# Attention values: query tiles outside and the two key tiles inside, with rows of V packed at 388 bytes

## The chip, the cores and the metric

One core of a Trainium2 chip runs the whole program. The metric is device time in microseconds (us), the median of repeated runs. A run's time is a little longer than the span of its profile, which goes from the first to the last instruction.

## What is computed

Inputs are bf16. There are 2048 query rows of width D = 640, 32 heads of width 192 with their own K and V of 2048 rows, and an FFN of width 1536.

```python
def _A_ref(x, k_cache, v_cache, wq, wo):
    q = (x @ wq).reshape(B, Sq, H, Dh).transpose(0, 2, 1, 3)
    scores = jnp.einsum("bhqd,bhkd->bhqk", q, k_cache) * (Dh ** -0.5)
    p = _softmax(scores, axis=-1)
    o = jnp.einsum("bhqk,bhkd->bhqd", p, v_cache)
    return o.transpose(0, 2, 1, 3).reshape(B, Sq, H * Dh) @ wo

xn = _layernorm(x)
s = _A_ref(xn, k_cache, v_cache, wq, wo)
g = _silu((_silu(xn @ w1) * (xn @ w3)) @ w2)
return x + s * g
```

## The kernel before

The program has a start (layer norm of x, turning it and the first K onto the contraction axis), a long attention part of some 1630 us, and an end (the rest of the FFN, then the product with wo for each of 16 query tiles). The order of instructions on each engine is the order in which the kernel text issues them.

The attention part walks a list of units, `stream`: 32 heads h, in each 4 query blocks qb of 512 queries, in each 8 units p of 256 keys; 1024 units in all. The loop at L653 issues for unit n the scores of unit n + 2 and then the values of unit n, so TensorE always has the scores of two units ahead in PSUM (`st2`) and in SBUF (`pT2`). At p = 0 it first issues the projection of one query block of the next head (`project`, L424: 20 matmuls).

- Scores (`emit_scores`, L487 and L488): six matmuls of 512 columns, two at a time: one on the upper 64 rows of the array and one on the lower 64, each into its own PSUM bank. ScalarE then takes exp of the 128 x 1024 result into `pT2` (L490): keys on partitions, and on the free axis two key tiles t of 512 queries each.
- Values (`values`, L503 to L527): for the two key tiles t and the four query tiles j of 128, and for the two row halves r of the array, one matmul at L516: stationary operand a 64 x 128 piece of `pT2`, moving operand 64 rows of V with 193 columns (192 of V and a column of ones, whose product is the softmax denominator), output the 193 columns of query tile j in `obanks[r]`. These are 16 matmuls in 8 pairs; the two of a pair (r = 0, 1) sit on different rows of the array and run together. `obanks[r]` is two PSUM banks: query tiles 0 and 1 lie in the first, 2 and 3 in the second. Each query tile gathers 16 products (8 units, two key tiles) in each row half. After the eighth unit of a block VectorE copies `obanks[0]` out (L525), adds `obanks[1]` (L526), and later divides by the denominator into `ostage` (L533).

V of a head lives in one of two SBUF tiles `vts[h % 2]`. A partition holds 16 key rows, one after the other. In the kernel before, each row has a place of 256 elements (512 bytes), of which 193 are used. The loads (`load_v`, L283): head 0's V comes in two halves, one from ScalarE's queue and one from SyncE's (L289); from head 1 on two DMAs a head on SyncE's queue (L292), one for the rows that go with t = 0 and one for t = 1, issued for head h + 2 when head h is through. Each row is a piece of 384 bytes. The column of ones is set once (L299).

SBUF tiles of the attention part are laid one behind the other in the order of their pools: `vts`, then `xnS`, `W`, `qA`, `qB`, `qC`, `pT2`, `ostage`, `pt`, `osum` and the layer norm's. When the part is over, the tiles of the end (`t`, `a`, L703 and L705, among them) take over that memory, and the first instruction that writes there waits for what was there before.

Of the kernel before, what the change touches and what calls it, by code (L numbers as in the profile page):

```python
# [11 lines left out]
BF16 = mybir.dt.bfloat16  # L12
# [3 lines left out]
P = 128  # L16
DH = 192
# [111 lines left out]
def _kernel_impl(  # L129
# [22 lines left out]
    NKT = SK // P  # L152
# [39 lines left out]
    vtp = att.enter_context(tc.tile_pool(name="vtp", bufs=1))  # L192
# [14 lines left out]
    xnS = xsp.tile([P, DC, SQ], BF16, name="xnS")  # L207
    x_all = fw.tile([P, WX], BF16, tag="xw", name="x_all")
    x_sb = x_all[:, 0:NQT * D].rearrange("p (t d) -> p t d", d=D)
    vts = [vtp.tile([P, NKT, 256], BF16, name=f"vt{i}") for i in range(2)]  # L210
    loads = {}

    def load_x(g, t0=0, t1=4, queue=nc.sync):
# [289 lines left out]
    def values(n):  # L503

        h, qb, p = stream[n]
        if p == 0:
            for r in range(2):
                obanks[r] = ps_o.tile([P, 1024], F32, tag=f"ob{r}", name=f"obank{r}")
        vt = loads[h]["vt"]
        pT2 = exps.pop(n)  # L510
        for t in range(2):
            for j in range(4):
                start = p == 0 and t == 0 and j % 2 == 0
                stop = p == NPAIR - 1 and t == 1 and j % 2 == 1
                for r in range(2):
                    nc.tensor.matmul(obanks[r][:, j * 256:j * 256 + DH + 1],  # L516
                                     lhsT=pT2[r * 64:(r + 1) * 64, t * 512 + j * P:t * 512 + (j + 1) * P],
                                     rhs=vt[r * 64:(r + 1) * 64, 2 * p + t, 0:DH + 1], start=start, stop=stop)
        if p < NPAIR - 1:
            return  # L520
        if h % HG == 0 and qb == 0:
            ostages[0] = stp.tile([P, NQT, HG * DH], BF16, tag="ostage", name="ostage")
        ov = [obanks[r][:].rearrange("p (j w) -> p j w", j=4)[:, :, 0:DH + 1] for r in range(2)]
        osum = osp.tile([P, 4, DH + 1], F32, tag="osum", name="osum")
        nc.vector.tensor_copy(out=osum[:], in_=ov[0])  # L525
        nc.vector.tensor_tensor(out=osum[:], in0=osum[:], in1=ov[1], op=ALU.add)  # L526
        osums[0] = osum  # L527
# [125 lines left out]
    for n, (h, qb, p) in enumerate(stream):  # L653
        if p == 0 and n > 0:
            if h + 1 < H:
                project(h + 1, qb)
            else:
                ffn_open(qb)
        if h == 0 and qb == 0 and p == 3:
            project(1, 0)  # L660
        if h == 0 and qb + 1 < NQB and p == (5 if qb == 0 else 4):
            project0(qb + 1)
        scores(n + 2)
        values(n)
        if p == 0 and n > 0:
            finish_block(n - 1)
        if p == (5 if h == 0 else 2) and h < 2 * NPIG:
            swiglu(h, qb)
        if p == 4 and h + 1 == H:
            ffn_close(qb)  # L670
        if h == 0:
            first_head(qb, p)
# [22 lines left out]
    for qb in range(NQB):  # L695
        qs = slice(qb * 512, (qb + 1) * 512)
        for fl in range(FL2 // P):
# [5 lines left out]
            t = fsb.tile([P, 512], BF16, tag="t", name="t")  # L703
# [19 lines left out]
    for i in range(NQT):  # L723
# [5 lines left out]
        for b, (c0, c1) in enumerate(DP):  # L729
            t = fsb.tile([P, 512], BF16, tag="ft", name="ft")  # L730
# [30 lines left out]
@with_exitstack  # L761
def kernel(
    ctx: ExitStack,
    tc: tile.TileContext,
    A_x: bass.AP,
    A_k_cache: bass.AP,
    A_v_cache: bass.AP,
    A_wq: bass.AP,
    A_wo: bass.AP,
    B_x: bass.AP,  # L770
    B_w1: bass.AP,
    B_w3: bass.AP,
    B_w2: bass.AP,
    out: bass.AP,
):
    _kernel_impl(ctx, tc, A_x, A_k_cache, A_v_cache, A_wq, A_wo, B_w1, B_w3, B_w2, out)
# [30 lines left out]
```

## Time and profile before

| what | value |
|---|---|
| median of 3 runs | 1939.32 us (1939.16 to 1939.7) |
| the profiled execution | 1939.16 us, its span 1937.4 us (1.76 us lie around it) |
| TensorE (matmuls) | busy 1927.5 us, 99% of the span |
| ScalarE | busy 1180.1 us, 61% |
| VectorE | busy 654.4 us, 34% |
| GpSimd | busy 282.4 us, 15% |
| values matmuls, L516 | 16384, 243 ns each from issue to end |
| V loads, L289 and L292 | 64 DMAs, median 6.0 us from issue to landing on SyncE's queue |

Matmuls are pipelined: the 243 ns of one is its way through the array. What sets the time is the step from one start to the next. Those steps are read from the chain of waits, which gives each group of matmuls the time until the next group starts, or from counts of matmuls in short windows.

### The profile page before, as it was taken

The numbers are of one execution on the slowest core, as the hardware profiler recorded it, in microseconds if no ns is written. First come the engines' busy times: TensorE is split into PE (matmuls) and PEld (weight loads), VectorE is DVE, ScalarE is ACT, GpSimd is POOL, SyncE is SP. The second block draws the span as 40 slices with busy tenths as digits, with TensorE's granted clock in tenths as the row PEclk, the third lists the DMA queues.
The fourth block names the chain that finished last, engine by engine and source line by source line (L and its number), as shares of the span: only waits on it lengthen the run. The fifth ranks groups of instructions, "written<-read, shape, count | busy, mean of one in ns | idle before, by whom it ended". The sixth has DMA issues, their size and how long they took to land.

```text
span 1937.4 us, 59668 instructions
## 1 busy us (share of the span) xinstructions
PE 1927.5 (99%) x27273; PEld 1316.9 (68%) x27281; DVE 654.4 (34%) x997; ACT 1180.1 (61%) x1278; POOL 282.4 (15%) x501
## 2 busy tenths in 40 slices
PE   9999999999999999999999999999999999999998
PEld 6666666666666666666666666666666666577776
DVE  7333333333333333333333333333333334521111
ACT  6667676767676767776777777677767677210000
POOL 3111111111111111111111111111111110000000
PEclk9999999999999999999999999999999999999999
DMA  8643433323333434363434343434334220937872
GB/s 179 131 101 66 100 68 80 88 60 89 59 88 64 98 64 98 68 162 68 101 64 101 69 101 69 101 64 100 69 67 97 59 68 2 251 76 138 152 151 62
DMA packets 394643, 178.98 MB, mean 92 GB/s; under 512 B 341616, under 2 KB 382832, under 8 KB 394384
## 3 DMA queue, kind: packets, MB, share of 16 engines
q1 hardware_dynamic: 371136, 125.32, 31.5%
q0 software_dynamic: 19472, 45.71, 10.1%
q8 instruction: 215, 3.52, 0.8%
q10 hardware_dynamic: 3776, 4.06, 0.7%
q14 instruction: 44, 0.36, 0.1%
HBM read 52.82 MB, written 27.79 MB: 42 GB/s over the span
## 4 chain that ended last, share of the span: by engine, by line
PE 98%; DMA 1%; DVE 1%; ACT 0%; SPq 0%; issue 0%; DVEq 0%; ACTq 0%
PE obank L516 35%; PE st L487 33%; PE ps L424 14%; PE ps_s L111 11%; PE ps_f L727 3%; PE ps_gu L701 1%; DMA x_all<-in_A_x_dram 1%; PE st L488 1%; PE ps L410 0%; DVE stats L316 0%; ACT KW L277 0%; PE pst L354 0%; ACT xnT L356 0%; DVE qA L429 0%; SPq L289 0%
## 5 line engine op out<-in xcount | busy, mean ns | idle before, releaser
L490 ACT ACTIVATE pT<-st 128x1024 bf16<-128x1024 f32 x1024 | 1046.2, 1022 | 250.9 <-PE st L488 235.3
L516 PEld LDWEIGHTS <-pT 64*128 64x128 bf16 x16384 | 711.6, 94 | 241.9 <-ACT pT L490 0.2
L516 PE MATMUL obank<-vt,pT 64*128 64x193 bf16 x16384 | 849.6, 243 | 0.0
L487 PE MATMUL st<-qC,KW 64*128 64x512 bf16 x2046 | 605.8, 376 | 0.1
L525 DVE COPY osum<-obank 128x772 f32<-128x772 f32 x128 | 123.1, 962 | 787.1 <-PE obank L516 787.1
L488 PE MATMUL st<-qB,KW 64*128 64x512 bf16 x1024 | 385.2, 376 | 0.0
L487 PE MATMUL st<-qA,KW 64*128 64x512 bf16 x1022 | 384.5, 376 | 0.4 <-ACT pT L490 0.3
L488 PE MATMUL st<-qC,KW 64*128 64x512 bf16 x1022 | 384.5, 376 | 0.0
L488 PE MATMUL st<-qA,KW 64*128 64x512 bf16 x1022 | 384.4, 376 | 0.0
L487 PEld LDWEIGHTS <-KW 64*128 64x128 bf16 x3068 | 278.5, 94 | 153.7 <-issue 2.1
L424 PE MATMUL ps<-xnT,W 64*128 64x512 bf16 x1280 | 297.2, 376 | 0.0
L424 PE MATMUL ps<-xnS,W 64*128 64x512 bf16 x1280 | 296.3, 376 | 0.0
L488 PEld LDWEIGHTS <-KW 64*128 64x128 bf16 x3068 | 278.8, 94 | 0.7 <-issue 0.6
L377 POOL DMA_DIRECT2D qC<-qA x124 | 65.4, 527 | 1284.5 <-DVE rl_all L532 1268.3
L430 ACT CAST qB<-ps 128x512 bf16<-128x512 f32 x131 | 76.7, 585 | 228.2 <-PE ps L424 222.7
L111 PE MATMUL ps_s<-wo_sb,oT 128*128 128x384 bf16 (+3 forms) x1535 | 208.8, 299 | 0.1
L424 PEld LDWEIGHTS <-W 64*128 64x128 bf16 x2560 | 123.1, 94 | 121.1
L111 PEld LDWEIGHTS <-oT 128*128 128x128 bf16 x1536 | 148.3, 98 | 60.5
L526 DVE TENSOR_TENSOR osum<-osum,obank 128x772 f32<-128x772 f32 x128 | 122.7, 959 | 13.4
L533 DVE TENSOR_TENSOR ostage<-osum,rl_all 128x768 bf16<-128x768 f32 x128 | 122.6, 958 | 6.2 <-DMA o_scr<-ostage 1.9
L465 DVE SCALAR_TENSOR_TENSOR hT<-pt,qB 64x512 bf16<-64x512 bf16 x64 | 43.8, 684 | 197.4 <-ACT pt L464 197.4
L429 DVE CAST qA<-ps 128x512 bf16<-128x512 f32 x131 | 90.6, 691 | 25.0 <-PE ps L410 7.2
(84 smaller groups left out, 623.7 us busy)
## 6 DMA issues: line engine op xcount, KB each, us to landing
o_scr<-ostage SPq DMA_DIRECT2D x16, 1536.0 KB, 10.6
vt<-in_A_v_cache_dram SPq DMA_DIRECT2D x63, 384.0 KB, 6.0
qC<-qA POOLq DMA_DIRECT2D x248, 64.0 KB, 1.9
qC<-qB POOLq DMA_DIRECT2D x124, 64.0 KB, 2.4
wo_sb<-in_A_wo_dram POOLq DMA_DIRECT2D x1, 7680.0 KB, 37.3
W<-in_A_wq_dram POOLq DMA_DIRECT2D x32, 160.0 KB, 3.6
W<-in_B_w_dram POOLq DMA_DIRECT2D x32, 80.0 KB, 3.3
W<-in_A_wq_dram POOLq DMA_DIRECT2D x32, 80.0 KB, 2.9
```

Source lines behind the costliest of these rows:

```text
L111: nc.tensor.matmul(ps[:, 0:w], lhsT=oT[:, k, :], rhs=wo_sb[:, k, c0:c1], start=(k == 0), stop=(k == OC - 1))
L377: nc.gpsimd.dma_start(out=qC[0:64, half, :], in_=qAB[half][64:P, :])
L424: nc.tensor.matmul(ps[:, r * 512:(r + 1) * 512], lhsT=W[rows, j, :], rhs=xs[rows, j // 2, qs], start=(j == 0), stop=(j == 2 * DC - 1))
L429: a = nc.vector.tensor_copy(out=qAB[0][:], in_=ps[:, 0:512])
L430: b = nc.scalar.copy(out=qAB[1][:], in_=ps[:, 512:1024])
L487: nc.tensor.matmul(st2[:, 0:512], lhsT=ka, rhs=qa, start=r == 0 and nr == 3, stop=r == nr - 1)
L488: nc.tensor.matmul(st2[:, 512:1024], lhsT=kb, rhs=qb2, start=r == 0 and nr == 3, stop=r == nr - 1)
L490: nc.scalar.activation(out=pT2[:], in_=st2[:], func=ACT.Exp, scale=att_scale)
L516: nc.tensor.matmul(obanks[r][:, j * 256:j * 256 + DH + 1], lhsT=pT2[r * 64:(r + 1) * 64, t * 512 + j * P:t * 512 + (j + 1) * P], rhs=vt[r ...
L525: nc.vector.tensor_copy(out=osum[:], in_=ov[0])
L526: nc.vector.tensor_tensor(out=osum[:], in0=osum[:], in1=ov[1], op=ALU.add)
L533: nc.vector.tensor_tensor(out=ostage[:, qb * 4:qb * 4 + 4, hg * DH:(hg + 1) * DH], in0=osum[:, :, 0:DH], in1=rl.unsqueeze(2).to_broadcast( ...
```

## The change

Two edits. `vts` is allocated with 194 elements a row (388 bytes) where it had 256 (512 bytes). In `values` the loops over query tiles j and key tiles t change places: all that belongs to one query tile is issued together, first with key tile 0, then with key tile 1. The inner loop over r, the operands and the number of the matmuls stay; `start` and `stop` still fall on the first and the last matmul into each bank.

```diff
-    vts = [vtp.tile([P, NKT, 256], BF16, name=f"vt{i}") for i in range(2)]
+    vts = [vtp.tile([P, NKT, DH + 2], BF16, name=f"vt{i}") for i in range(2)]
```
```diff
-        for t in range(2):
-            for j in range(4):
+        for j in range(4):
+            for t in range(2):
                 start = p == 0 and t == 0 and j % 2 == 0
                 stop = p == NPAIR - 1 and t == 1 and j % 2 == 1
                 for r in range(2):
```

In the built programs the two tiles of V take 2 x 6208 bytes a partition in place of 2 x 8192, and the tiles behind them in SBUF lie 3968 bytes lower. The instructions of every engine stand in the same order as before, but for the order of the eight pairs. Three waits differ. In the first unit of each of heads 1 to 31 the wait for the load of the t = 1 rows stands on the second pair of matmuls; it stood on the fifth. The first ACTIVATE of L704 also waits for five earlier loads of weights into `W`, and the first instruction of L706 for four, because `t` and `a` now lie where `W` was.

## The prediction

> **What bounds the kernel now.** I read the page first: its engine shares, its clock row and its chain by line.
>
> ```profile
> PE 1927.5 (99%) x27273; PEld 1316.9 (68%) x27281; DVE 654.4 (34%) x997; ACT 1180.1 (61%) x1278; POOL 282.4 (15%) x501
> PEclk9999999999999999999999999999999999999999
> PE 98%; DMA 1%; DVE 1%; ACT 0%; SPq 0%; issue 0%; DVEq 0%; ACTq 0%
> PE obank L516 35%; PE st L487 33%; PE ps L424 14%; PE ps_s L111 11%; PE ps_f L727 3%; PE ps_gu L701 1%; DMA x_all<-in_A_x_dram 1%; PE st L488 1%; PE ps L410 0%; DVE stats L316 0%; ACT KW L277 0%; PE pst L354 0%; ACT xnT L356 0%; DVE qA L429 0%; SPq L289 0%
> ```
>
> TensorE is the bound from end to end, at its full granted clock, and the line that the change reorders holds 35% of the chain: nothing waits in front of it. So the question is whether a values unit (16 matmuls) takes longer or shorter. The costliest groups confirm that these matmuls stand idle for nothing:
>
> ```profile
> L516 PEld LDWEIGHTS <-pT 64*128 64x128 bf16 x16384 | 711.6, 94 | 241.9 <-ACT pT L490 0.2
> L516 PE MATMUL obank<-vt,pT 64*128 64x193 bf16 x16384 | 849.6, 243 | 0.0
> ```
>
> Third, the chain in order of time in the middle of the attention part (start, length, what):
>
> ```profile
> 903.03 0.67 PE obank L516 x16
> 903.70 0.21 PE st L487
> ...
> 904.35 0.67 PE obank L516 x16
> 905.01 0.21 PE st L487
> ...
> 905.66 0.67 PE obank L516 x16
> ```
>
> A unit repeats every 1.31 us: three rounds of scores and 0.67 us for 8 pairs of values, 83 ns a pair. Fourth, one unit looked into: windows that all begin at 902.80 us and end ever later, with the matmuls of L516 counted in brackets behind TensorE's busy time.
>
> ```profile
> 902.80:902.96 0.16, 0.09 (x4) 0.09 (x4) 1.00 0.00 0
> 902.80:903.04 0.24, 0.17 (x6) 0.17 (x5) 1.00 0.00 0
> 902.80:903.13 0.33, 0.26 (x8) 0.26 (x8) 1.00 0.00 0
> 902.80:903.21 0.41, 0.34 (x10) 0.34 (x10) 1.00 0.23 50
> 902.80:903.30 0.50, 0.43 (x12) 0.43 (x12) 1.00 0.43 98
> ```
>
> Each 0.08 to 0.09 us brings one more pair. In this order the output bank changes behind the second and sixth pair and, between the fourth and fifth, both the bank and the row of V; no step is longer. From the start times of the trace, averaged over 1021 units, the second matmul of a pair starts 3.5 ns behind the first and the next pair 79.9 ns behind that; the step over the change of row is 79.87, the others 79.85 to 79.89. A pair costs 83.3 ns.
>
> **The change part by part.** *Order of the pairs, values.* Removed and added: nothing; 16 matmuls and 16 weight loads a unit stay. Three things move. (a) The row of V now changes at every pair and not once: 0 by the step just shown. (b) The output bank changes once inside a unit, not three times: 0 by the same row. (c) A query tile's two key tiles are now added into the same 193 PSUM columns in consecutive pairs, 83.3 ns apart; before, three other pairs lay between. The kernel has rows for back-to-back sums into the same columns: the last output tile's narrow piece at L111 adds 48 products of 128 columns, all into the same place. Windows of it:
>
> ```profile
> 1930.00:1931.00 1.00, 1.00 (x21) 1.00 (x19) 1.00 0.00 0
> 1930.00:1932.00 2.00, 2.00 (x39) 2.00 (x37) 1.00 0.00 0
> ```
>
> The second microsecond brings 18 matmuls: 55.6 ns each, narrower and closer than 83.3, and with no stall. That piece uses the whole array and not its halves; the scores do use the halves, add three times into one place and also run at their 215.8 ns a round. So (c) is 0. Upper bound: if a sum had to wait until the former one is through (243 ns in place of 83.3), 160 ns on 4096 of the 8192 pairs would be 655 us; the 128-column row (219 ns each, 55.6 apart) speaks against it, and I take 0. Weight loads (94 ns, in pairs on two halves) step through `pT2` in another order and stay hidden under the matmuls.
>
> *Pitch of V.* What can a row starting at a multiple of 388 bytes cost the moving operand? No matmul of this trace streams from such a start, so the price is bounded. The steps give the stream's grain: 215.8 ns for 512 columns and 55.8 for 128 (from the start times) make 0.4167 ns a column and 2.5 ns fixed. 193 columns would be 82.9; measured 83.3, which is 194. I read this as two columns, 4 bytes, at a time, 0.83 ns; 388 is a multiple of 4, so no row needs one more. Low end 0: there is nothing to gain, since pairs already run at the step of a 194-column stream. High end: one more grain on each pair, 8192 x 0.83 = 6.8 us. I take 0, the grain being the nearest row, and keep 6.8 for the range.
>
> [...]
>
> *The V loads.* The same 64 DMAs of the same 384-byte pieces, now onto packed rows. From head 2 on V is loaded a whole head (50.7 us) ahead and lands in about 6 us; head 1's is issued at 60.7 us, lands by about 67 and is read from 75 us: 7 us of cover. If a load took 8 us longer, TensorE would stand in front of head 1 for one. The first half of head 0's V is issued at 6.39 us, lands 7.1 us later, and is read at 16.02: 2.5 us of cover. The tight place is the second half:
>
> ```profile
> 12.43 1.18 SPq L289 DMA_DIRECT2D vt<-in_A_v_cache_dram  x1
> 13.65 1.56 SPq L214 DMA_DIRECT2D x_all<-in_A_x_dram  x1
> 21.97 0.89 DVE L316 BATCH_NORM_STATS2 stats<-x_all 128x6 f32<-128x320 bf16 x2 [0.60 <-DMA x_all<-in_A_x_dram]
> 23.71 0.73 PE L354 MATMUL pst<-ident_bf,xn 128*128 128x128 bf16 x10 [0.75 <-DVE qA L429]
> 25.04 0.83 PE L516 MATMUL obank<-vt,pT 64*128 64x193 bf16 x16
> ```
>
> V itself lands at 20.3 us and is first read at 25.04. But x's third group is queued behind it on SyncE; VectorE waits for that at 21.97, the cast of L429 stands behind VectorE's wait, and TensorE's transposes behind the cast. Every microsecond by which V is slower arrives there. Its 64 pieces on each of 16 DMA engines took 22 ns for most pieces of this size in the records and 42 to 48 for the slowest twentieth, so the bounds are 0 and, were all slow, 64 x 22 = 1.4 us. I take 0.3, nearer to the plain pieces.
>
> *Waits and addresses.* In 31 units the wait for the t = 1 rows stands three pairs (0.25 us) earlier on TensorE, with all of its stream queued behind it. The load is over by 8 us (head 1) or some 40 us (later heads): 0; uncovered it would be 31 x 0.25 = 7.8 us. The new waits of L704 and L706 near 1647 us are for loads whose last was issued at 1588.6 and took 3.4 us: 0. The tiles that lie 3968 bytes lower keep 64-byte starts, and the rows of their instructions have no reason to change: 0. The memset of the ones is one of 72 ns for each tile, as before.
>
> Sum: 1939.16 (its span 1937.4 and 1.76 around it) + 0 + 0 + 0.3 = 1939.46; the profiled execution lies 0.16 below the median of the runs, which gives 1939.6.
>
> **The rivals.** *1, the other side: a misaligned row start costs every values pair a fixed slot.* Place: the moving operand's stream at L516, on the chain. Price 0.83 ns a pair and 6.8 us in all, 1946.1; two grains would give 1953. For it: no aligned row can refute it, and 35% of the chain would pay. Against it: the grain of 4 bytes. It decides from 0.48 ns a pair (3.9 us over 8192). *2: sums into the same columns stall when they follow each other in half-array mode.* Only the second pair of each query tile would pay: one fixed slot of 2.5 ns on 4096 pairs is 10.2 us, 1949.5. Against it stand L111 and the scores. *3: faster.* If bank changes cost something that the steps hide, say the spread of 0.04 ns between them on two changes of 1024 units, it is 0.1 us; to pass 0.2% it would need 3.9 us, while all that TensorE stands idle is 9.9 us (1937.4 - 1927.5), most of it before head 0's second block, where the change can only delay. *4: the change doesn't do what it says.* The order does change in the built program, and the pitch too; what doesn't follow is that anything on the chain cares. That is the forecast itself. Within it, a start delayed by the full 1.4 us gives 1940.9.
>
> **How the numbers follow.** A measurement here can tell about 0.2% (3.9 us) from no change. Forecast, no change, 1937.5 to 1942: 0.62. Rival 1: 0.25 and rival 2: 0.07, nearly all above 0.2%. Faster by more than 0.2%: 0.06. So faster 0.06, same 0.62, slower 0.32. The range goes down to 1937.5 and up to 1947.5: it takes in the one-grain price and leaves out the larger prices of rivals 1 and 2 (about 0.13) and the faster case (0.06).
>
> **What would show it.** In the changed profile: units every 1.31 us and 0.67 us for 16 matmuls in the chain; a pair step of 83.3 ns, evenly spaced. Rival 1: a longer step on all eight pairs, 84.1 ns for one grain, or on rows with certain offsets. Rival 2: long and short steps in turn, the long one in front of each query tile's second key tile. Start: VectorE's wait for x at 21.97 us moved by the slower V pieces. The forecast is wrong if the pair step moves by 0.5 ns or more, or if the chain shows something other than TensorE in the attention part.

## The result and the profile after

The changed kernel takes 1947.25 us (median of 6 runs, 1946.97 to 1948.81) against 1939.39 for the kernel before (6 runs): a ratio of 1.0042, 95% interval 1.0029 to 1.0055. That is 7.9 us slower. The profiled execution has a span of 1945.2 us, 7.8 more than before.

The page names the same bound as before, and the same shares:

```profile
PE 1935.1 (99%) x27273; PEld 1323.2 (68%) x27281; DVE 654.4 (34%) x997; ACT 1180.2 (61%) x1278; POOL 282.6 (15%) x501
PEclk9999999999999999999999999999999999999999
PE 98%; DMA 1%; DVE 1%; ACT 0%; SPq 0%; issue 0%; DVEq 0%; ACTq 0%
L516 PE MATMUL obank<-vt,pT 64*128 64x193 bf16 x16384 | 857.7, 243 | 0.0
```

TensorE's busy time grew by 7.6 us, at the same clock and with the same number of matmuls; what used to wait for it waits longer (ScalarE's exp at L490 242.1 us in all, 235.3 before). A matmul of L516 still takes 243 ns from issue to end, so that figure hides the change. The chain in order of time shows it as a longer period of the blocks. Before:

```profile
75.25 2.16 PE ps L424 x20
87.93 2.16 PE ps L424 x20
100.60 2.16 PE ps L424 x20
```

After:

```profile
88.11 2.16 PE ps L424 x20
100.84 2.16 PE ps L424 x20
```

Each such row opens a query block with its projection. A block took 12.67 us and takes 12.73; 0.06 us on each of 128 blocks is the 8 us. Inside a unit, the same count of L516 in windows with one beginning (902.20 us, after):

```profile
902.20:902.34 0.14, 0.09 (x4) 0.09 (x3) 1.00 0.00 0
902.20:902.42 0.22, 0.17 (x4) 0.17 (x4) 1.00 0.00 0
902.20:902.43 0.23, 0.18 (x6) 0.18 (x6) 1.00 0.00 0
902.20:902.51 0.31, 0.26 (x8) 0.26 (x7) 1.00 0.00 0
902.20:902.59 0.39, 0.34 (x8) 0.34 (x8) 1.00 0.00 0
902.20:902.60 0.40, 0.35 (x10) 0.35 (x10) 1.00 0.00 0
```

The second pair has started by 902.34 and the third has not by 902.42; the fourth has by 902.51 and the fifth not by 902.59. Windows in steps of 10 ns are too coarse to say more; by their start times the eight pairs of this unit lie 83, 87, 83, 87, 81, 87 and 82 ns apart. The steps are uneven now. Averaged over the units of heads 1 to 30, from the start times (ns from the start of a pair to the start of what follows it; the last column is the mean of the three rounds of scores that come next):

```
pair          1      2      3      4      5      6      7      8     sum   scores
before      83.3   83.4   83.3   83.3   83.4   83.3   83.3   83.3   666.7   215.8
after       83.3   87.5   82.5   86.2   82.5   86.1   82.5   86.1   676.8   215.2
```

Pairs 2, 4, 6 and 8 are those with key tile 1. They take 2.8 to 4.2 ns more; every step behind a slow one, the scores included, takes some 0.7 to 0.8 ns less. The values of a unit lose 10.1 ns and its scores win 2.0 back: 8.1 ns on 1024 units, 8.3 us. The projections win some 0.2 ns on each of their 10 rounds a block, 0.3 us in all. That makes 8.0, against 7.8 measured. The start, the end and all waits off TensorE have no part in it.

### The profile page after: what moved, and what is told of

Read it like the earlier page. It is cut to its first block, busy times and chain, and to the rows that moved or that the text cites. A ratio compares the mean times of both kernels' runs of the same rounds, so it can differ in the third digit from the quotient of the medians.

```text
span 1945.2 us, 59672 instructions
## 1 busy us (share of the span) xinstructions
PE 1935.1 (99%) x27273; PEld 1323.2 (68%) x27281; DVE 654.4 (34%) x997; ACT 1180.2 (61%) x1278; POOL 282.6 (15%) x501
## 4 chain that ended last, share of the span: by engine, by line
PE 98%; DMA 1%; DVE 1%; ACT 0%; SPq 0%; issue 0%; DVEq 0%; ACTq 0%
PE obank L516 35%; PE st L487 33%; PE ps L424 14%; PE ps_s L111 11%; PE ps_f L727 3%; PE ps_gu L701 1%; DMA x_all<-in_A_x_dram 1%; PE st L488 1%; PE ps L410 0%; DVE stats L316 0%; ACT KW L277 0%; PE pst L354 0%; ACT xnT L356 0%; SPq L289 0%; DVE qA L429 0%
## 5 line engine op out<-in xcount | busy, mean ns | idle before, releaser
L490 ACT ACTIVATE pT<-st 128x1024 bf16<-128x1024 f32 x1024 | 1046.2, 1022 | 257.7 <-PE st L488 242.1
L516 PEld LDWEIGHTS <-pT 64*128 64x128 bf16 x16384 | 717.7, 94 | 242.3 <-ACT pT L490 0.2
L516 PE MATMUL obank<-vt,pT 64*128 64x193 bf16 x16384 | 857.7, 243 | 0.0
```

Source lines behind the costliest of these rows:

```text
L490: nc.scalar.activation(out=pT2[:], in_=st2[:], func=ACT.Exp, scale=att_scale)
L516: nc.tensor.matmul(obanks[r][:, j * 256:j * 256 + DH + 1], lhsT=pT2[r * 64:(r + 1) * 64, t * 512 + j * P:t * 512 + (j + 1) * P], rhs=vt[r ...
```

## The experiments

The pattern has two candidate causes, one for each edit, and the possibility that it takes both. The first four runs undo one edit or change its size.

**e1, the pitch alone** (the kernel before, with this edit):

```diff
-    vts = [vtp.tile([P, NKT, 256], BF16, name=f"vt{i}") for i in range(2)]
+    vts = [vtp.tile([P, NKT, DH + 2], BF16, name=f"vt{i}") for i in range(2)]
```

> Pitch 388 with the old order (t outside, j inside). In the changed kernel each pair with the second key tile (odd key row, which starts at an odd multiple of 4 bytes) takes 86 to 87.5 ns to the next pair's start, each with the first key tile 82.5 to 83.3, against 83.3 everywhere before. Theory P (a row that starts at an odd multiple of 4 bytes costs the stream 3 to 4 ns): pairs 5 to 8 of a unit are slow, pairs 1 to 4 are not, a unit takes about 677 ns, time about 1947 us (ratio 1.004). Theory O (two sums into the same columns in consecutive pairs cost it): no change, 83.3 ns on all pairs, 1939 us (ratio 1.000). Theory C (only both together, a row change at each pair and unaligned rows): only the fifth pair differs, 0.5 to 1 us, 1940 us.

Measured: 1941.5 us against 1939.48 (ratio 1.0009, interval 1.0 to 1.0018). Only the fifth pair is slow. The count of L516 in windows of e1:

```profile
902.20:902.63 0.43, 0.34 (x10) 0.34 (x10) 1.00 0.00 0
902.20:902.71 0.51, 0.42 (x10) 0.42 (x10) 1.00 0.00 0
902.20:902.72 0.52, 0.43 (x12) 0.43 (x12) 1.00 0.00 0
```

Five pairs have started by 902.63, and the sixth, due 83 ns behind the fifth's 902.62, only between 902.71 and 902.72. The means of the eight steps are 83.3 four times, then 87.5, 82.5, 82.5 and 82.8: 2.0 ns a unit, 2.0 us in 1024 units, which is the measured difference. Pairs 6 to 8 stream key tile 1 as well and are not slow, so theory P in its plain form (an unaligned row costs) falls. The place is the one that theory C named, the step from one row to another; its size for the single step, 0.5 to 1 us, was too small.

**e2, the order alone** (pitch 512, j outside and t inside).

> The new order with the old pitch of 512 bytes. Theory P: 83.3 ns on all pairs, 1939 us (ratio 1.000). Theory O: slow and fast pairs in turn as in the changed kernel, a unit 677 ns, 1947 us (ratio 1.004). Theory C: 1939 us.

Measured: 1939.58 us (ratio 1.0, 0.9991 to 1.0009); 83.3 ns on all eight steps. At this pitch two consecutive sums into the same PSUM columns cost nothing. Theory O falls, and the order by itself is free.

**e3, rows at 392 bytes**, in the new order (`DH + 4`).

> The changed kernel with rows of V at 392 bytes, so that every row starts at a multiple of 8 bytes and all else is as in the change. Theory P with a grain of 8 bytes: 83.3 ns on all pairs, 1939 us. Theory P with a grain of 16 bytes or more: a mean between. Theory O: as the changed kernel, 1947 us.

Measured: 1946.66 us (ratio 1.0036, 1.0022 to 1.005); steps as in the changed kernel (87.5, then 86.1). Here key tile 1's rows start 8 bytes behind a multiple of 16 bytes and key tile 0's at one; in the changed kernel they start 4 and 12 bytes behind one, and 0 and 8. The slow steps stay with key tile 1 whatever the offset of key tile 0. An offset of 8 bytes is slow here, with key tile 1 (87.5 and 86.1 ns), and not in the changed kernel, where key tile 0's rows start there in every second unit (82.3 to 83.1 ns in those units). So it is not the alignment of a row, but which row comes after which.

**e4, one other pair between the two sums** (pitch 512):

```diff
-        for t in range(2):
-            for j in range(4):
+        for j, t in ((0, 0), (1, 0), (0, 1), (1, 1), (2, 0), (3, 0), (2, 1), (3, 1)):
+            if True:
```

> Pitch 512, and within each output bank the order query tiles a, b with key tile 0 and then a, b with key tile 1: the two sums into the same columns have one other pair between them. Theory O: if one pair between is enough, 83.3 ns on all pairs and 1939 us; if not, about as the changed kernel. Theory P: 1939 us.

Measured: 1939.47 us (ratio 1.0001, 0.9992 to 1.001), 83.3 ns on all steps. With e2 it takes PSUM off the list.

**p1, the cost by itself.** What remains is a step from a row to its neighbour in SBUF. This probe takes the rest of the kernel away and runs 16 layouts one after the other: 32 units each of three rounds of scores and 16 values matmuls on TensorE, no other engine at work once the inputs are loaded, and no attention result. It was run once, like p2 and p3, so each figure of the three is a mean over the units of one execution. Its rows are given by functions:

```python
def rows(pitch, gap=1, shift=0):
    return lambda p, t: (2 * p + t if gap == 1 else t * gap + p) * pitch + shift * t
...
    ("v388", rows(194), JT, W, W),
    ("v388t", rows(194), TJ, W, W),
    ("v388apart", rows(194, gap=8), JT, W, W),
    ("v400", rows(200), JT, W, W),
```

> The disputed cost by itself: TensorE alone runs units of the same shape (three rounds of scores, 8 pairs of values) on 16 layouts of the moving operand, 32 units each; no exp, softmax or projections, and the output is not the reference's. So far: at 388 and 392 bytes the slow pair goes from key tile 0's row to key tile 1's, its neighbour in SBUF (87.5 ns at the first in a unit, 86.1 later); the way back costs nothing at any offset, nor does any pair at 512. Theory A (neighbours: a stream that begins in the memory line where the last one ended pays about 4 ns): 512 none; 388, 386 slow; 388 with t outside one slow pair a unit; 388 with rows eight apart none; 388 backwards slow only where the next query tile's first row follows; 388 with 128 columns, ending 132 bytes ahead of the next row, none; of 400 to 480 those slow whose next row shares a line with the last one's end: none with lines of 16 bytes, 400 with 32, 400 to 432 with 64; 512 with key tile 1's stream 4 or 32 bytes into its row none; a stream starting inside the last none; one that starts at a multiple of 512 where the last ended none. Theory D (a step of the start address that is not a multiple of some power of two): 388, 386, 388 apart, 388 with 128 columns and 512 with 4 bytes off all slow; which of 400 to 480 are slow gives the power. Theory S (a start inside or just behind what the last stream read): the last two cases are slow too.

Measured, ns from the start of a pair to the next, and of the whole unit with its scores (without the first units, in which the pace hasn't settled):

```
case          1      2      3      4      5      6      7      8     unit
v512        83.3   83.3   83.3   83.3   83.3   83.3   83.3   83.3   1314.2
v388        83.5   87.3   82.7   86.1   82.6   86.3   82.5   86.1   1322.3
v388t       83.3   83.3   83.3   83.3   87.5   82.5   82.5   82.8   1316.1
v388apart   83.3   83.3   83.3   83.3   83.3   83.3   83.3   83.3   1314.2
v388back    83.1   83.8   87.1   82.9   85.7   82.6   86.2   82.0   1320.0
v386        83.2   87.6   82.4   87.2   82.5   86.8   82.5   86.8   1325.1
v400        83.3   83.3   83.3   83.3   83.3   83.3   83.3   83.3   1314.1
v512off4    83.3   85.0   82.5   82.5   83.3   85.0   82.5   82.5   1314.2
```

416, 432, 448 and 480 bytes, a shift by 32 bytes, and a second stream that starts 128 bytes into the first are all at 1314.1 to 1314.2. The first three rows reproduce the kernels of 512, of the change and of e1 within 0.3 ns a step. v388 starts at 53.7 us, when the inputs have landed, and from there on nothing but TensorE runs inside a case: neither DMA nor another engine has part in it (on the probe's page VectorE, GpSimd and DMA are at 0 tenths from the fourth of 40 slices to the last but one). The group of one case by its tile, in the probe, also shows that the 243 ns of a matmul is no measure of this:

```profile
L92 PE MATMUL ob<-v388apart,pt x512: 240/243/254, 139.8 to 181.7; 64*128 64x193 bf16 x171
L92 PE MATMUL ob<-v388back,pt x512: 241/243/253, 182.6 to 224.7; 64*128 64x193 bf16 x171
```

Same length of each, but 41.9 us from first to last start in one and 42.1 in the other.

With the same pitch of 388, rows eight apart are free; and 400 bytes are free while 386 to 392 are not. That speaks for theory A with lines of 16 bytes: at 400 the next row starts in a fresh line, at 386, 388 and 392 in the line where the former row's 386th byte lies. Against A stood one case: a stream from byte 126 to 511 and then one from 512, which A has as free, took 1320.0 (`vnextline`; its steps are 84.0, 84.0, 87.0, 82.0, 86.0, 82.0, 86.0 and 83.0). 388 with 128 columns, whose streams end well ahead of the next, took 1095.8 a unit, where eight steps of 55.8 and three rounds of scores make 1094: nearly none, as A has it.

**p2, where exactly the second row starts.** The same probe, key tile 0's row at byte 0 (a, c) or 10 (b) of its place, key tile 1's at the byte in the name:

```python
def two(a, b):
    return lambda p, t: p * 512 + (a, b)[t]
...
    ("a398", two(0, 199), JT, 193, 193),
    ("a400", two(0, 200), JT, 193, 193),
    ("b396", two(5, 198), JT, 193, 193),
    ("c194at388", two(0, 194), JT, 194, 194),
```

> The same probe (TensorE alone, scores and values of the same shape, output not the reference's) with 16 other pairs of rows: key tile 0's row starts at byte 0 (cases a, c) or 10 (cases b) of a place of 1024 bytes, key tile 1's where the case's name says. The first probe: 386, 388 slow (a unit 677 to 679 ns), 400 to 480 and rows apart 666.7, and slow too where a stream from byte 126 to 511 is followed by one from 512. Theory A16 (lines of 16 bytes, slow if the next stream starts in the line of the last stream's last byte): a386 to a398 slow, a400 and a402 666.7; b396 slow, b400 to b416 666.7; of c only 194 columns at 388 slow. It misses the stream from 126. Theory R16 (streams are fetched 16 bytes at a time counted from their own start, slow if the next stream starts in a line that the last of these fetches touches): as A16 in a and c, but b396, b400, b408 and b412 all slow, b416 not. Theory G (slow if the gap between the streams is under some 10 bytes): a386 to a394 slow; b396 and b400 slow, b412 and b416 not; of c 192 at 384, 192 at 388, 194 at 388 and 200 at 400 all slow. The same row twice (last case): 666.7 in all three.

Measured, ns a unit:

```
a386 1324.5   a390 1324.4   a394 1324.4   a398 1325.0   a400 1314.1   a402 1317.5
b396 1322.2   b400 1317.5   b408 1317.5   b412 1317.5   b416 1317.5
c 192 columns at 384: 1307.5   192 at 388: 1307.5   194 at 388: 1321.7   200 at 400: 1334.2   193, same row twice: 1314.2
```

Theory A16 fits. Its line is here the 16 bytes from a multiple of 16 on, as the steps show it; what it is in the memory the runs don't tell. The step down lies between 398 (1325.0) and 400 (1314.1), where the second row leaves the line of bytes 384 to 399 in which the first one's last byte lies. With key tile 0's row moved by 10 bytes it lies between 396 (1322.2) and 400 (1317.5), again at the line and not at a fixed distance (theory G) nor 16 bytes behind the first row's end (theory R16: 400 to 412 would be slow like 396). 192 columns at 384 bytes follow without a gap and are not slow (1307.5, eight steps of 82.5 and the scores): the former row ends with its line. 200 columns at 400 took 1334.2; eight steps of 200 x 0.4167 + 2.5 ns, the prediction's estimate for a stream that nothing disturbs, and three rounds of scores at 215.8 make 1334.1. The rest, 1317.5, A16 doesn't have: it expected 1314 there. These are the cases with a row that starts at a place that is no multiple of 4 bytes (10, or 402) and shares no line; they show a second, smaller cost of 3.4 ns a unit, whatever the gap. Rows that start 4, 8 or 12 bytes into a line and share none don't show it (`v388apart`, 1314.2). The odd case of p1 may belong here: its slow steps are those of the pairs that start at byte 126, not those that start at 512. But its 5.8 ns a unit are more than 3.4, and no run takes this second cost apart.

**p3, a new row at each step**, and the whole array in place of its halves.

```python
def seq(pitch):
    return lambda k, r: k * pitch
```

> The probe with a new row at each step (pair k of a unit streams row k), in half-array pairs and with the whole array (16 matmuls of 128 rows, row 2k + r); output not the reference's. The second probe fitted one rule: a pair is slow when its stream starts in the 16-byte line in which the stream before it ended (87.5 ns for 83.3), and a later step wins 0.8 ns back. If the rule holds, half512 and half400 take 666.7 ns a unit; half388 pays on seven of eight pairs and has no quiet pair to win back on: 667 + 7 x 4.2 = 696 ns; if the price is paid only once and then kept in flight, nearer 677. With only the upper or only the lower half's rows packed: the same as half388 if the halves are bound together, half of it if they aren't. Whole array: full512 and full400 83.3 ns a matmul; full388 87.5 on 15 of 16 if the rule is one of the memory, 83.3 if it is one of the half-array mode.

Measured: half-array 512 and 400 bytes 666.7 ns each for the eight pairs; 388 bytes 683.2, with steps 83.3, 87.6, 85.8, 85.9, 82.4, 86.2, 85.7, 86.3. The fifth step is quiet (82.4): the row that starts at 4 x 388 = 1552 = 97 x 16 begins a fresh line. Whole array: 83.3 a matmul inside a unit at 512 and 400 bytes; at 388, from the second on, 88.0, 85.1, 85.9, 83.0, 86.0, 85.1, 85.9, 83.0 and so on, quiet at every fourth (83.0), where the row starts at a multiple of 16. So it is not one of the half-array mode. The price a step is 4.2 ns only for the first one; when it is paid again at once it is 2 to 3, less than the 7 x 4.2 expected.

In two more cases only one half's rows are packed. There the halves no longer keep step, so pairs can't be told by the order of the starts; each half has to be followed by itself. The first round of scores on the upper half (L65) and on the lower one (L66), in a unit near the start of the case `half388upper` and in the unit 21 later:

```profile
142.53 0.37 PE L65 MATMUL st<-q,kw 64*128 64x512 bf16 x1
142.57 0.38 PE L66 MATMUL st<-q,kw 64*128 64x512 bf16 x1
...
170.18 0.38 PE L66 MATMUL st<-q,kw 64*128 64x512 bf16 x1
170.42 0.37 PE L65 MATMUL st<-q,kw 64*128 64x512 bf16 x1
```

The upper half, whose rows are packed, took 27.89 us for 21 units: 1328.3 ns each, as with both halves packed. The lower one took 1314.2 a unit, as at 512 bytes, and got 14 ns further ahead with each, until it led by 239 ns; from there on it took 1328 too. With the lower half's rows packed it is the other way round, up to a lead of 324 ns. So each half pays for its own stream, and the other one pays nothing until it has run ahead that far. What sets the lead the runs don't tell.

Four runs of the whole kernel that were to test the line there gave no result: the new order with rows at 400, 416 and 448 bytes, and at 388 with key tile 1's row eight rows behind key tile 0's. That 400 bytes would bring it back to 1939 us rests on p1.

## Why the prediction was wrong

Its forecast, no change, failed in one step: "*Pitch of V* ... I take 0, the grain being the nearest row". The part's estimate of a 4-byte grain fits p2, where 192 columns take 82.5 ns a pair and 193 take 83.3, as 194 would by its 0.4167 ns a column and 2.5 fixed. But it looked at each row by itself: does it start unaligned? The runs show that the cost lies between two rows: at 388 bytes the next row starts in the line of 16 bytes in which the last one ended, and that step takes 87.5 or 86.1 ns in place of 83.3, four times in a unit. The measured 1947.25 lies inside the stated range, 0.25 us under its top; the top was set by the price of a lost grain on every pair, which is not what happened, so this is luck.

- *Order, (a), (b) and (c)*: right at the pitch at which they were read. e2 and e4 measure 0 for all three. But (a), "the row of V now changes at every pair ... 0 by the step just shown", took a step measured at 512 bytes as the price at 388. That step is the one that costs. The two edits were priced one by one: e1 gives 2.0 us for the pitch, e2 0 for the order, and both together give 7.9, because the order sets how often a unit steps from a row to its neighbour: once (e1), or four times.
- *The bound from above*, one grain on each pair, 6.8 us, was none: 7.9 were measured, and of another make: 2.8 to 4.2 ns on every second pair, less what is won back.
- *Rival 1* had the right engine, line and order of magnitude (1946.1 for 1947.25) and the wrong place: it expected all eight pairs alike at 84.1, or rows with certain offsets, which e1 and e3 rule out. *Rival 2* had the right picture, "long and short steps in turn, the long one in front of each query tile's second key tile", for a cause, sums into the same columns, that e2 rules out; the long step is that of the second key tile's pair itself.
- *The V loads*: the 0.3 us for a slower start was not there. V's second half again landed 7.9 us behind its issue, and VectorE's wait for x moved from 21.97 to 21.90 us:

```profile
21.90 0.89 DVE L316 BATCH_NORM_STATS2 stats<-x_all 128x6 f32<-128x320 bf16 x2 [0.54 <-DMA x_all<-in_A_x_dram]
23.64 0.73 PE L354 MATMUL pst<-ident_bf,xn 128*128 128x128 bf16 x10 [0.67 <-DVE qA L429]
```

  Packed rows didn't slow the loads: on SyncE's queue they land in a median of 5.5 us in the profile after, 6.0 in the one before. A V piece of 384 bytes took 31 ns in the median before, where 22 was the commonest value (41% of the pieces) and not that of most, and 22 in the median after. Head 1's V is first read at 78.06 us in the chain before, not at 75, where the block's projection stands; its cover is larger than was said, and nothing rests on it.
- *Waits and addresses*: right; no new wait shows on any engine.

## What to carry to other kernels

Where TensorE streams one short row after another, pad the rows so that the next one starts in a fresh 16-byte line: in the probes, with rows of 193 columns, 400 bytes did all that 512 did (1314.1 and 1314.2 ns a unit), and 386 to 398 cost 0.6 to 0.8% of a unit; in the whole kernel 388 and 392 cost 0.4%. Price two edits together when one sets how often the other's step is taken: here 2.0 and 0 us apart made 7.9. And look for such a cost in the distances between starts, not in the length of an instruction (243 ns) or in busy shares (TensorE 99%), which both stayed as they were.

## What the runs showed that was not expected

A slow step is partly won back: the steps behind it run at 82.5 for 83.3 ns, scores right behind the values at 215.1 for 215.8, below the pace that TensorE holds undisturbed for a whole kernel. A disturbance of 1.7 ns (v512off4) was won back whole within two steps, 83.3 + 85.0 + 82.5 + 82.5 = 333.3. What this reserve is, the runs don't tell. And the two halves of the array keep their own time: the second matmul of a pair starts 3.5 ns behind the first in the whole kernel and 65 to 72 in most cases of p1, at the same steps, and in p3 one half ran up to 324 ns ahead of the other that paid.
